# Writing a kernel's converted weights to a tile of their own in one pass, and issuing the next raw load right behind it

## The chip, the cores and the metric

The kernel runs on one core of a Trainium2 chip. The metric is the device time of one execution in microseconds (us). Engines are TensorE (PE, with its weight loads PEld), VectorE (DVE), ScalarE (ACT), GpSimd (POOL) and SyncE (SP), which here only issues DMAs.

## The reference, cut to what matters

```python
scores = np.matmul(q, k.transpose(0, 1, 3, 2)) / np.sqrt(D)        # 8 images, 8 heads, 576 x 64
scores = np.where(mask, scores + bias, -1e9)                       # window of 128 positions
attn = np.exp(scores - max); attn = attn / (attn.sum() + 1e-9)
x = np.matmul(attn, v)                                             # as 4608 x 512
h = np.maximum(np.maximum(x @ w1, x @ w2), x @ w3)                 # 512 x 768 each
out = h @ w_out                                                    # 768 x 512
```

q, k and v are 32-bit floats. The four weight matrices reach the kernel as 64-bit floats; their bits are made into 32-bit floats on the chip.

## The kernel before, in words

**Work by image.** Each of the 8 images has 18 attention steps (two heads of 128 rows each). In a step the scores are computed on PE (L431), masked and biased on DVE (L447 or L450, then L461 twice), exponentiated on ACT (L473 twice), summed and inverted (ACT L479, DVE L480), scaled on POOL (L487) or ACT (L492), transposed on PE (L500), copied out of PSUM by ACT (L504, L509 or L512), masked on POOL (L520, L524) and multiplied with v on PE (L545, later L567). ACT's L552 takes the finished head out.

The x of a finished image is cut into a high and a low part (ACT L614, DVE L615). Then PE makes the maxout products, image after image, while the attention of the next image is worked in between. Image 0 is done in 44 plain units, v = 0 to 43, each of 12 matmuls of 128x288 (L791; the first half of units 0 to 2 stands apart as L767). Four units make one of the groups g = 0 to 8 of w1, w2, w3. The results lie in three PSUM banks used in turn, so unit v can begin only when the result of unit v - 3 has been taken out: by ACT (L805) or by DVE (L808), depending on g. Image 0's units begin at about 57.5 us, and from there PE has work to the end.

**The weights.** They come in 12 sets of 128 x 1024 values in the order of `g_order`; "set n" below is the n-th in that order (sets 0, 1 and 5 to 11 serve g = 0 to 8, sets 2 to 4 the output matrix). For each set `preparing` does this:

- `fetch` (L152) loads the raw 64-bit words into one of two buffers (`raw_tile`, name hs2) over SP's queue.
- `exponents` works on the exponent bytes: one DVE pass (L166) for the first six sets, two ACT passes (L170, L171) for the others.
- `convert` makes sign and exponent with one DVE pass (L177 or L181) and joins them with the mantissa by a shift and an or (L186).
- The floats are stored to DRAM (L327, `plain`), and `part` cuts them in two steps into a high part (ACT L200) and a low part (DVE L203) in `ring` or `ow`, from which PE reads, and stores those (L216, `keep`).

In the kernel before, L186 writes the floats over the front of the raw buffer. Its output starts where the small exponents lay, and it goes in three passes of 256, 512 and 256 elements. The buffer is then free only when the floats have been stored and both parts made, and the fetch of set n + 2 is written behind the second part (L333).

**What sets the order.** Up to image 2 a scheduler decides at compile time in which order each engine takes its instructions; the events list gives only the order in which they are written. Each engine and each DMA queue then works its own list strictly in order, waiting on semaphores. What stands behind a waiting instruction waits too.

The pool of 7 buffers named hs also holds `dist`, `idle` and, from group 2 on, the cut h of an image.

Of the kernel before, what the change touches and what calls it, by code (L numbers as in the profile page):

```python
# [8 lines left out]
F32 = mybir.dt.float32  # L9
F32R = mybir.dt.float32r  # L10
I32 = mybir.dt.int32
U32 = mybir.dt.uint32
# [3 lines left out]
ALU = mybir.AluOpType  # L16
# [21 lines left out]
def attention_maxout_kernel(  # L38
# [11 lines left out]
    nc = tc.nc  # L50
    P = 128
# [3 lines left out]
    DM = H * D  # L55
    NG = w_all.shape[0]
# [12 lines left out]
    hs_p = ctx.enter_context(tc.tile_pool(name="hs_p", bufs=7))  # L69
# [21 lines left out]
    for a in range(2):  # L91
        for d in (slice(0, P),) if a == 0 else (slice(0, D), slice(D, P)):
            nc.gpsimd.affine_select(
                out=prev[d, a], in_=prev[d, a], pattern=[[1, P]], compare_op=ALU.is_gt, fill=0.0,
# [49 lines left out]
    raws = {}  # L144
    SMALL = DM // 2

    def raw_tile():
        return hs_p.tile([P, SMALL + 4 * DM], I32, name="hs2", bufs=2)

    def fetch(g):  # L150
        r = raws[g] = raw_tile()
        nc.sync.dma_start(r[:, SMALL:].bitcast(U8)[:, :16 * DM - 3], w_all[g].bitcast(U8)[:, 3:])  # L152

    def pieces(g):
        r = raws[g]
        x = r[:, SMALL:].rearrange("p (n w) -> p n w", w=2)
        sign = r[:, SMALL:].bitcast(I8).rearrange("p (n b) -> p n b", b=8)[:, :, 4]
        return x[:, :, 0], x[:, :, 1], sign, r[:, :SMALL].bitcast(I8)

    def floats(g):  # L160
        return raws[g][:, :2 * DM].bitcast(F32).rearrange("p (e w) -> p e w", e=4)

    def exponents(g, few):
        _, t, top, small = pieces(g)
        if few:
            x = nc.vector.tensor_scalar(out=small, in0=top, scalar1=-56.0, scalar2=56.0, op0=ALU.max, op1=ALU.min)  # L166
            if g == 0:
                tc.keep_in_program_order(x)
        else:
            nc.scalar.activation(small, top, AF.Relu, bias=-56.0)  # L170
            nc.scalar.activation(t.bitcast(F32), top, AF.Relu, scale=-2.0 ** 27, bias=-56.0 * 2.0 ** 27)  # L171

    def convert(g, few):
        u, t, top, small = pieces(g)
        u = u.bitcast(U32)
        if few:
            nc.vector.tensor_tensor_reduce(  # L177
                out=t, in0=top, in1=small, scale=2.0 ** 27, scalar=0.0, op0=ALU.subtract, op1=ALU.max, accum_out=None,
            )
        else:  # L180
            nc.vector.scalar_tensor_tensor(  # L181
                out=t, in0=small, scalar=2.0 ** 27, in1=t.bitcast(F32), op0=ALU.mult, op1=ALU.subtract
            )
        y = raws[g][:, :2 * DM].bitcast(U32)
        for c in (slice(0, SMALL), slice(SMALL, 3 * SMALL), slice(3 * SMALL, 4 * SMALL)):
            nc.vector.scalar_tensor_tensor(  # L186
                out=y[:, c], in0=u[:, c], scalar=5, in1=t[:, c].bitcast(U32),
                op0=ALU.logical_shift_right, op1=ALU.bitwise_or,
            )

    def sums(t, n):
        for to, a, b, op in (
# [17 lines left out]
    def part(g, n):  # L210
        e = slice(2 * n, 2 * n + 2)
        if g < 9:
            f = plain_place(g)
            hi_lo(f[:, e, 0], f[:, e, 1], floats(g)[:, e])
            k = slice(1, 4) if n else slice(0, 1)
            nc.sync.dma_start(keep[g][n][:, :k.stop - k.start], f[:, k].bitcast(F32))  # L216
        else:
            f = ow[:, slice(5, 7) if n else slice(0, 5, 4), g - 9]
            hi_lo(f[:, :, 0], f[:, :, 1], floats(g)[:, e])
# [64 lines left out]
    def ahead(n, a):  # L284
        if (n, a) in SPARE:
            return begun == B and (n < LAST + 8 or made == B)
        if n < 9 * PB:
            return n < 3 or (n - 3, 3) in used
        i = ringed[a].index(n)
        if i < 9 * PB + RING:  # L290
            return all((x, 3) in used for x in range(i - 3, i - 1))
        return i < RING or (ringed[a][i - RING], 6 if a else 3) in used
# [27 lines left out]
    g_order = [0, 1, 9, 10, 11, 2, 3, 4, 5, 6, 7, 8]  # L320

    def preparing():
        for n, g in enumerate(g_order):
            exponents(g, n < FEW)
            yield
            convert(g, n < FEW)
            nc.sync.dma_start(plain_keep[g], floats(g))  # L327
            yield
            for k in range(2):
                while g < 9 and not ahead(g, 1):  # L330
                    yield True
                part(g, k)
                if k == 1 and n + 2 < NG:  # L333
                    fetch(g_order[n + 2])
                yield

    prepared, owed = 0, 0
    steps_of_weights = preparing()

    def weights(n=0, upto=0):  # L340
# [269 lines left out]
    xs, hs, hq = {}, {}, {}  # L610
# [266 lines left out]
    for s, (t, i) in enumerate(steps):  # L877
        c = s + shift[tasks[t][0]]
# [16 lines left out]
    for t, (b, _) in enumerate(tasks):  # L895
        for e in sorted(set(MIX[t % 4])):
            c = where[t, e]
# [92 lines left out]
```

## Time and profile before

| | before |
|---|---|
| median of 3 runs | 750.51 us (749.09 to 750.65) |
| the profiled execution, its own time | 752.57 us |
| its span in the profile | 750.9 us |
| PE busy | 733.9 us, 98% of the span |
| DVE busy | 515.2 us, 69% |
| ACT busy | 487.2 us, 65% |
| POOL busy | 236.4 us, 31% |
| raw weight loads | 12 of 1023.6 KB, 7.2 us median to landing |

The span is what the profiler sees between the first and the last instruction; the time contains some launch cost around it. The profiled execution is 2.06 us above the median of the runs.

### The profile page before, as it was taken

The numbers are of one execution on the slowest core, as the hardware profiler recorded it, in microseconds if no ns is written. First come the engines' busy times: TensorE is split into PE (matmuls) and PEld (weight loads), VectorE is DVE, ScalarE is ACT, GpSimd is POOL, SyncE is SP. The second block draws the span as 40 slices with busy tenths as digits, with TensorE's granted clock in tenths as the row PEclk, the third lists the DMA queues.
The fourth block names the chain that finished last, engine by engine and source line by source line (L and its number), as shares of the span: only waits on it lengthen the run. The fifth ranks groups of instructions, "written<-read, shape, count | busy, mean of one in ns | idle before, by whom it ended". The sixth has DMA issues, their size and how long they took to land.

```text
span 750.9 us, 19281 instructions
## 1 busy us (share of the span) xinstructions
PE 733.9 (98%) x7209; PEld 674.6 (90%) x7214; DVE 515.2 (69%) x1614; ACT 487.2 (65%) x1603; POOL 236.4 (31%) x451
## 2 busy tenths in 40 slices
PE   7999989999999999999999999999999999999998
PEld 3459988999999999999999999999999999999998
DVE  4888887536659477784778567794777747683673
ACT  5786976766667767676677757776666767552342
POOL 4661224645556123212222123222222122343100
PEclk8999999999999999999999999999999999999999
DMA  7877999759998489855988378864988468899611
GB/s 252 274 282 298 330 340 331 253 187 340 361 349 275 134 279 303 273 181 192 322 294 276 116 266 304 291 213 146 330 289 273 163 228 272 252 291 355 230 61 64
DMA packets 57085, 192.81 MB, mean 257 GB/s; under 512 B 5792, under 2 KB 24480, under 8 KB 50464
## 3 DMA queue, kind: packets, MB, share of 16 engines
q0 software_dynamic: 20304, 108.54, 43.9%
q1 hardware_dynamic: 36400, 82.85, 31.2%
q8 instruction: 57, 0.93, 0.5%
q14 instruction: 36, 0.29, 0.1%
q10 hardware_dynamic: 288, 0.20, 0.1%
HBM read 156.95 MB, written 34.60 MB: 255 GB/s over the span
## 4 chain that ended last, share of the span: by engine, by line
PE 77%; DVE 11%; ACT 7%; DMA 2%; issue 1%; POOL 1%; SPq 0%; DVEq 0%; ACTq 0%; POOLq 0%
PE ps_m L846 46%; PE ps_m L791 16%; PE ps_s L431 5%; PE pt L500 4%; PE ps_x L567 4%; DVE hs L615 2%; DVE hq L733 2%; ACT p L473 2%; DVE t L732 2%; DMA qk<-in_qk 1%; PE ps_x L545 1%; DMA hs<-in_w_all 1%; ACT p L492 1%; DVE t L618 1%; DVE xs L615 1%
## 5 line engine op out<-in xcount | busy, mean ns | idle before, releaser
L846 PE MATMUL ps_m<-xs,ring 128*128 128x288 f32 x2160 | 302.7, 297 | 0.6
L846 PEld LDWEIGHTS ps_m<-xs,ring 128*128 128x128 f32 x2160 | 290.1, 188 | 3.7 <-ACT t L863 3.4
L520 POOL TENSOR_SCALAR_AFFINE_SELECT pp<-pr 128x256 f32<-128x256 f32 x112 | 53.9, 482 | 277.2 <-ACT pr L504 154.0
L473 ACT ACTIVATE p<-s,st 128x128 f32<-128x128 f32 x288 | 114.7, 400 | 20.8 <-DVE st L461 17.2
L863 ACT COPY t<-ps_m 128x288 f32<-128x288 f32 x196 | 76.7, 394 | 71.2 <-PE ps_m L846 69.5
L791 PE MATMUL ps_m<-xs,ring 128*128 128x288 f32 x846 | 118.1, 297 | 2.8 <-DVE hq L808 2.2
L791 PEld LDWEIGHTS ps_m<-xs,ring 128*128 128x128 f32 x846 | 113.3, 188 | 4.1 <-DVE hq L808 2.4
L367 POOL DMA_DIRECT2D ring<-keep x103 | 55.5, 539 | 165.5 <-PE ps_m L846 157.3
L846 PE MATMUL ps_m<-hs,ow 128*128 128x288 f32 x756 | 105.8, 297 | 0.4
L846 PEld LDWEIGHTS ps_m<-hs,ow 128*128 128x128 f32 x756 | 100.9, 188 | 2.6 <-ACT t L863 1.2
L492 ACT ACTIVATE p<-p,st 128x128 f32<-128x128 f32 x252 | 84.6, 393 | 24.1 <-DVE st L480 24.1
L732 DVE TENSOR_TENSOR t<-ps_m,t 128x288 f32<-128x288 f32 x108 | 48.8, 453 | 42.8 <-PE ps_m L846 32.5
L461 DVE CUSTOM_DVE_ANT_0 s<-ps_s,bias 128x128 f32<-128x128 f32 x240 | 60.6, 285 | 9.0 <-POOL bias_t L112 3.4
L431 PE MATMUL ps_s<-qk 64*64 64x192 f32 (+1 forms) x1088 | 62.0, 319 | 3.4 <-DMA qk<-in_qk 2.4
L614 ACT CAST hs<-hq 128x288 fp32r<-128x288 f32 x96 | 40.2, 432 | 30.8 <-DVE hq L733 18.1
L473 ACT ACTIVATION_READ_ACCUMULATOR p<-s,st 128x1 f32 x288 | 55.3, 192 | 0.0
L567 PE MATMUL ps_x<-pp,v 64*64 64x64 f32 (+3 forms) x1456 | 53.4, 274 | 0.1
L567 PEld LDWEIGHTS ps_x<-pp,v 64*64 64x64 f32 x1456 | 41.7, 133 | 10.5 <-issue 8.6
L500 PE MATMUL pt<-plus,p 128*128 128x128 f32 x288 | 48.5, 289 | 2.0 <-POOL p L487 1.3
L524 POOL TENSOR_SCALAR_AFFINE_SELECT pp<-pr 128x256 f32<-128x256 f32 (+1 forms) x112 | 50.0, 447 | 1.1
L733 DVE TENSOR_TENSOR hq<-t,hq 128x288 f32<-128x288 f32 x108 | 48.8, 457 | 2.1
L601 DVE TENSOR_TENSOR xk<-ps_x,xk 128x256 f32<-128x256 f32 (+3 forms) x56 | 25.4, 454 | 36.0 <-ACT xk L600 36.0
(94 smaller groups left out, 942.0 us busy)
## 6 DMA issues: line engine op xcount, KB each, us to landing
ring<-keep POOLq DMA_DIRECT2D x51, 1024.0 KB, 7.4
ring<-keep POOLq DMA_DIRECT2D x61, 768.0 KB, 6.1
qk<-in_qk SPq DMA_DIRECT2D x31, 576.0 KB, 5.3
hs<-in_w_all SPq DMA_DIRECT2D x12, 1023.6 KB, 7.2
v<-in_v SPq DMA_DIRECT2D x32, 320.0 KB, 6.5
outT<-t SPq DMA_DIRECT2D x64, 144.0 KB, 1.8
keep<-ring SPq DMA_DIRECT2D x9, 768.0 KB, 6.5
plain<-hs SPq DMA_DIRECT2D x12, 512.0 KB, 4.0
```

Of the source, the lines that this page charges most:

```text
L367: nc.gpsimd.dma_start(wts[n, a], keep[n % 9][a])
L431: pe(nc.tensor.matmul(ps[j][d:d + D, o:o + k1 - k0], lhsT=qkt[u][j * D:(j + 1) * D, 0, q0:q0 + D], rhs=qkt[u][j * D:(j + 1) * D, 1, k0:k1] ...
L461: first(nc.vector.tensor_tensor_reduce(out=x, in0=ps[j][:, P:2 * P], in1=below, scale=-0.125, scalar=3.0e38, op0=ALU.add, op1=ALU.min, acc ...
L473: nc.scalar.activation(p[:, j], x, AF.Exp, bias=st[:, 0, a, j:j + 1], scale=-1.0, accum_out=st[:, 1, a, j:j + 1])
L492: nc.scalar.activation(p[:, j], p[:, j], AF.Copy, scale=st[:, 2, a, j:j + 1])
L500: pe(nc.tensor.transpose(out=pt[:, a, j], in_=p[:, j], identity=ident))
L567: pe(nc.tensor.matmul(x[j * D:(j + 1) * D, r, o:o + rhs.shape[1]], lhsT=vv[k, i, j * D:(j + 1) * D], rhs=rhs[k], start=start, stop=True, s ...
L732: nc.vector.tensor_tensor(out=s, in0=ps, in1=e, op=ALU.add)
L733: nc.vector.tensor_tensor(out=h, in0=s, in1=h, op=ALU.max)
L791: pe(nc.tensor.matmul(ps, lhsT=lt, rhs=rt, start=n == 0 and not (b == 0 and v < EARLY), stop=n == len(pairs) - 1, skip_group_check=True,))
L846: pe(nc.tensor.matmul(part_of[n, {2: 0, 5: 0, 6: 0, 3: 1}.get(kk, kk)], lhsT=lt, rhs=rt, start=first, stop=i == len(pairs) - 1, skip_group ...
L863: nc.scalar.copy(out=e, in_=ps)
```

## The change

The floats get a tile of their own from the pool hs. Because nothing is overwritten now, one pass of 1024 elements takes the place of the three. The fetch of the set after the next is written directly behind the pass, ahead of the store of the floats; it has to wait only for the passes that read the raw buffer.

```diff
+    made_floats = {}
+
     def floats(g):
-        return raws[g][:, :2 * DM].bitcast(F32).rearrange("p (e w) -> p e w", e=4)
+        return made_floats[g].rearrange("p (e w) -> p e w", e=4)
...
-        y = raws[g][:, :2 * DM].bitcast(U32)
-        for c in (slice(0, SMALL), slice(SMALL, 3 * SMALL), slice(3 * SMALL, 4 * SMALL)):
-            nc.vector.scalar_tensor_tensor(
-                out=y[:, c], in0=u[:, c], scalar=5, in1=t[:, c].bitcast(U32),
-                op0=ALU.logical_shift_right, op1=ALU.bitwise_or,
-            )
+        made_floats[g] = hs_p.tile([P, 2 * DM], F32, name="hs")
+        nc.vector.scalar_tensor_tensor(
+            out=made_floats[g].bitcast(U32), in0=u, scalar=5, in1=t.bitcast(U32),
+            op0=ALU.logical_shift_right, op1=ALU.bitwise_or,
+        )
...
             convert(g, n < FEW)
+            if n + 2 < NG:
+                fetch(g_order[n + 2])
             nc.sync.dma_start(plain_keep[g], floats(g))
...
                 part(g, k)
-                if k == 1 and n + 2 < NG:
-                    fetch(g_order[n + 2])
```

The scheduler answers with another order on every engine. Three places matter below. In the changed kernel's rows the line numbers are higher by 1 (up to the fetch) or 2 to 3 within `convert` (L183 is L181 of before, L187 the one pass).

The first place is SP's list at set 0, near the program's start (plain0 and keep0 are the stores of group 0, hs2 the raw buffers). Before:

```order
L327 DMA plain0_138<-hs2_161 128x1024
L216 DMA keep0_0_120<-ring_119 128x512
L216 DMA keep0_1_121<-ring_119 128x1536
L152 DMA hs2_354<-in_w_all 128x8189
L399 DMA v_364<-in_v 128x640
```

With the change:

```order
L152 DMA hs2_335<-in_w_all 128x8189
L330 DMA plain0_138<-hs_333 128x1024
L217 DMA keep0_0_120<-ring_119 128x512
L217 DMA keep0_1_121<-ring_119 128x1536
L400 DMA v_363<-in_v 128x640
```

The load of set 2 moved from behind the three stores of set 0 to ahead of them; it is so for each later set.

The second place is DVE's list around the drain of unit v = 20 (the last row of each piece: ps_m2_1476 before, ps_m2_1466 with the change, hold that unit's result). Before, the raw buffer hs2_1087 holds set 9:

```order
L181 SCALAR_TENSOR_TENSOR hs2_1087<-hs2_1087 128x1024
L480 RECIPROCAL st_1359<-st_1359 128x4
L186 SCALAR_TENSOR_TENSOR hs2_1087<-hs2_1087 128x256
L601 TENSOR_TENSOR xk0_1219<-ps_x_1435,xk0_1219 128x256
L186 SCALAR_TENSOR_TENSOR hs2_1087<-hs2_1087 128x512
L450 COPY_PREDICATED ps_s_102<-prev_108,ps_s_102 128x2x128
L186 SCALAR_TENSOR_TENSOR hs2_1087<-hs2_1087 128x256
L461 ISA s_1472,st_1471<-ps_s_102,bias_113 128x128
...
L203 TENSOR_TENSOR ring_119<-hs2_1087,ring_119 128x2x256 x2
L461 ISA s_1474,st_1471<-ps_s_102,bias_113 128x128
...
L808 TENSOR_TENSOR hq_1181<-ps_m2_1476,hq_1181 128x288
```

With the change, hs2_1159 holds set 10:

```order
L183 SCALAR_TENSOR_TENSOR hs2_1159<-hs2_1159 128x1024
L187 SCALAR_TENSOR_TENSOR hs_1468<-hs2_1159 128x1024
L602 TENSOR_TENSOR xk0_1212<-ps_x_1425,xk0_1212 128x256
L451 COPY_PREDICATED ps_s_102<-prev_108,ps_s_102 128x2x128
L204 TENSOR_TENSOR ring_119<-hs_1468,ring_119 128x2x256
L462 ISA s_1462,st_1461<-ps_s_102,bias_113 128x128
...
L462 ISA s_1464,st_1461<-ps_s_102,bias_113 128x128
...
L204 TENSOR_TENSOR ring_119<-hs_1468,ring_119 128x2x256
L809 TENSOR_TENSOR hq_1174<-ps_m2_1466,hq_1174 128x288
```

The same work stands ahead of the drain, but it belongs to the next set: the weights run one set further ahead, and L480 has left the stretch.

The third place is ACT's list while image 0's attention is still running (ow is where set 2's parts go, pr is filled from the transposed attention, xk_445 is the finished head that L552 takes out). Before:

```order
L552 COPY xk_445<-ps_x 128x576
L473 ACTIVATE p,st<-s,st 128x128
L504 COPY pr<-pt 128x512
L200 CAST ow<-hs_354 128x2x256 x2
L473 ACTIVATE p,st<-s,st 128x128 x2
L479 ACTIVATE st<-st 128x4
```

With the change:

```order
L553 COPY xk_445<-ps_x 128x576
L201 CAST ow<-hs 128x2x256 x2
L474 ACTIVATE p,st<-s,st 128x128 x2
L505 COPY pr<-pt 128x512
L480 ACTIVATE st<-st 128x4
```

The two casts of set 2 and one more exponential now stand ahead of the copy of the transposed attention.

## Rows read from the trace of the kernel before

**Rows 1.** Busy time by stretch: PE, PEld, DVE, ACT, POOL; clock, DMA share, GB/s.
```profile
97.00:123.33 26.33, 22.43 (x247) 20.25 (x245) 21.67 (x63) 20.84 (x60) 9.35 (x15) 1.00 0.93 329
123.33:751.00 627.67, 623.11 (x6203) 593.32 (x6201) 417.89 (x1304) 394.70 (x1308) 186.28 (x362) 1.00 0.74 248
```

**Rows 2.** Timeline of PE: start, length, instructions, idle before them.
```profile
42.85 2.66 PE L767 MATMUL ps_m<-xs,ring 128*128 128x288 f32 x18 [0.18 <-DVE xs L615]
...
57.52 4.27 PE L791 MATMUL ps_m<-xs,ring 128*128 128x288 f32 x30 [0.63 <-DVE xs L615]
...
96.94 5.03 PE L791 MATMUL ps_m<-xs,ring 128*128 128x288 f32 x36
104.14 1.86 PE L791 MATMUL ps_m<-xs,ring 128*128 128x288 f32 x12 [2.17 <-DVE hq L808]
...
115.02 0.88 PE L431 MATMUL ps_s<-qk 64*64 64x192 f32 x16 [0.95 <-DVE st L461]
...
122.73 0.84 PE L500 MATMUL pt<-plus,p 128*128 128x128 f32 x4 [0.64 <-ACT p L492]
```

**Rows 3.** Timeline of DVE around the drain of unit 20.
```profile
98.50 1.23 DVE L181 SCALAR_TENSOR_TENSOR hs<-hs 128x1024 int32<-128x1024 int8 x1 [2.11 <-ACT hs L171]
...
102.01 1.49 DVE L203 TENSOR_TENSOR ring<-hs,ring 128x512 fp32r<-128x512 f32 x2
...
103.64 0.45 DVE L808 TENSOR_TENSOR hq<-ps_m,hq 128x288 f32<-128x288 f32 x1
```

**Rows 4.** Timeline of ACT: the exponent passes of sets 6, 7 and 9.
```profile
67.91 1.15 ACT L170 ACTIVATE hs<-hs 128x1024 int8<-128x1024 int8 x1 [1.32 <-DMA hs<-in_w_all]
...
78.09 1.15 ACT L170 ACTIVATE hs<-hs 128x1024 int8<-128x1024 int8 x1 [0.46 <-DMA hs<-in_w_all]
...
97.36 1.11 ACT L171 ACTIVATE hs<-hs 128x1024 f32<-128x1024 int8 x1
```

**Rows 5.** The page's group of exponentials: count | busy, mean ns | idle before.
```profile
L473 ACT ACTIVATE p<-s,st 128x128 f32<-128x128 f32 x288 | 114.7, 400 | 20.8 <-DVE st L461 17.2
```

**Rows 6.** Waits of SP's queue to 140 us: total, times, longest.
```profile
SPq L152 <- DMA plain<-hs: 15.7, 8, 3.2
```

**Rows 7.** The raw loads (line L152), from issue to landing.
```profile
DMA to landing us min/median/max: 5.0/7.2/10.7
```

**Rows 8.** Timeline of DVE: passes of set 1 and what follows the first.
```profile
28.25 0.42 DVE L186 SCALAR_TENSOR_TENSOR hs<-hs 128x256 uint32<-128x256 uint32 x1
28.58 0.29 DVE L447 COPY_PREDICATED ps_m<-prev,ps_m 128x128 f32<-128x128 uint8 x1
28.78 0.68 DVE L186 SCALAR_TENSOR_TENSOR hs<-hs 128x512 uint32<-128x512 uint32 x1
```

**Rows 9.** Timeline of ACT in image 0's attention.
```profile
38.43 0.57 ACT L504 COPY pr<-pt 128x512 f32<-128x512 f32 x1
38.89 1.14 ACT L200 CAST ow<-hs 128x512 fp32r<-128x512 f32 x2
...
45.76 0.59 ACT L504 COPY pr<-pt 128x512 f32<-128x512 f32 x1
```

**Rows 10.** Timeline of DVE in image 0's attention.
```profile
33.51 0.69 DVE L166 TENSOR_SCALAR hs<-hs 128x1024 int8<-128x1024 int8 x1
...
34.41 1.28 DVE L177 CUSTOM_DVE_ANT_0 hs<-hs 128x1024 int32<-128x1024 int8 x1
...
47.39 0.18 DVE L480 RECIPROCAL st<-st 128x4 f32<-128x4 f32 x1
...
56.30 1.17 DVE L615 TENSOR_TENSOR xs<-xk,xs 128x576 fp32r<-128x576 f32 x1
```

**Rows 11.** Timeline of POOL in image 0's attention.
```profile
34.56 1.40 POOL L524 TENSOR_SCALAR_AFFINE_SELECT pp<-pr 128x256 f32<-128x256 f32 x1
...
39.43 0.41 POOL L524 TENSOR_SCALAR_AFFINE_SELECT pp<-pr 128x256 f32<-128x256 f32 x1
...
49.60 0.61 POOL L487 TENSOR_TENSOR p<-p,st 128x256 f32<-128x256 f32 x1
```

## The prediction

> **What bounds the kernel now.** I first read the busy times by stretch. From 123.33 us to the end PE is busy for 623.11 of 627.67 us at a granted clock of 1.00, full speed; nothing the change touches runs there, so that part moves as one block. Between 97 and 123.33 us PE is busy for only 22.43 of 26.33 us, and this is where the weights are still being made [rows 1]. So the time is: when image 0's units begin (57.52 us), plus PE's work, plus what PE waits after that.
>
> PE's timeline names these waits. There are three between 57.52 and 123.33 us: 2.17 us before unit 23, released by DVE's L808; 0.95 us before a score block, released by DVE's L461; 0.64 us before a transposition, released by ACT's L492 [rows 2]. Together they are 3.76 us, the most that the later stretch can give. PE also waited 0.63 us just before 57.52 us.
>
> The timeline of DVE says why unit 23 waits. Unit 23 needs the bank of unit 20, whose drain ran at 103.64 us, although PE began units 20 to 22 at 96.94 us. The drain stood behind the whole of set 9: DVE sat idle for 2.11 us for ACT's exponent pass L171, ran L181 at 98.50 us, then the passes, two L203 from 102.01 us, and only then the drain [rows 2, 3]. The exponent pass on ACT, at 97.36 us, waited for no load. But ACT and DVE release each other in turn from 78 us on, and that round began late: ACT waited for raw loads, 1.32 us for set 6 and 0.46 us for set 7 [rows 4]. The loads were late because SP held them behind the stores: the raw fetch waited 15.7 us in 8 waits for the store of the floats [rows 6].
>
> **The change part by part.**
>
> *One pass for three.* A pass of 256 elements takes 0.42 us, and the next instruction starts 0.33 us after it; one of 512 takes 0.68 us, of which I count 0.60 us to the next start by the same overlap [rows 8]. That makes 0.27 us per 256 elements and 0.06 us fixed, so 1024 elements in one pass cost about 1.14 us of DVE against 0.33 + 0.60 + 0.33 = 1.26 us. It saves 0.12 us a set, 1.4 us in 12 sets. L181, an operation of the same kind on 1024 elements, took 1.23 us with its tail [rows 3], which agrees. Only the sets ahead of a PE wait can hand it on: I count two of them, 0.2 us. The lower bound is nothing (DVE waits for ACT in the round anyhow), the upper 0.4 us.
>
> The first cast of a set (ACT L200) needed only two of the passes before and needs all of the one now. But other work stood between the passes, and L480 and L601 leave that stretch in the new order, so I cost it at nothing.
>
> *Two tiles instead of one.* The new tile comes from the pool hs. By then the cut h of group 2 takes four of its seven buffers. A pass could wait for the store of an older set's floats, but the sets come some 10 us apart (67.91 and 78.09 us [rows 4]), and with three buffers left the store has two sets' time to land. I cost it at nothing; if a store took longer than that, the pass and every drain behind it on DVE would wait for the rest.
>
> *The earlier fetch.* It passes the store of its set's predecessor and, for ring sets, two keep stores. Those stores stand one instruction further back, and nobody waits for them before image 1. The load takes 5.0 to 10.7 us [rows 7] and now starts when the raw words were last read, not when the floats have been stored and cut. ACT's two waits for loads, 1.32 and 0.46 us, go. More than that: the order shows that with the loads in time the scheduler puts the weights one whole set ahead. Where set 9 stood ahead of unit 20's drain, set 10 stands now; set 11, which was made from 114 us on, takes the place of set 10, and behind it no weights are left.
>
> *What this does to PE's waits.* The second and third wait, 0.95 and 0.64 us, lay where DVE and ACT made sets 10 and 11. With set 11 a place earlier, ACT and DVE have only attention and drains there, and I let both waits go: -1.59 us. The first wait stays in part, since a set still stands ahead of unit 20's drain. The round on ACT and DVE begins 0.46 us earlier (no wait for the load) and loses some 0.2 us by the merged passes, and behind L181 only one exchange with ACT is left ahead of the drain, where L480, an extra pass and a second exchange stood. From L181's start to the drain was 103.64 - 98.50 = 5.14 us; without the passes' 0.12 us and one L480 and wait I take 4.6 us. So the drain comes 0.46 + 0.54 = 1.0 us earlier, and the first wait falls from 2.17 to about 1.2 us. Bounds: nothing (the round is paced by something else) and the whole 2.17 us.
>
> *What it does to the start.* The new order also brings weights forward into image 0's attention, and here it costs. Set 2's two casts, 1.14 us [rows 9], and one exponential, 0.40 us [rows 5], now stand ahead of ACT's L504, which ran at 38.43 us: this copy comes 1.5 us later. On DVE all of set 3 (L166 0.69, L177 1.28, the pass 1.14 us [rows 8, 10]) moves ahead of the last score steps, which come some 3 us later. Three things give back. The 18 matmuls of L767, 2.66 us, stood ahead of a transposition and now stand behind it [rows 2], so the next L504 (45.76 us [rows 9]) comes earlier. The last L480 ran at 47.39 us, but POOL's L487, which needs it, only at 49.60 us [rows 10, 11]: 2.2 of the 3 us are slack. And the last L615, at 56.30 us, no longer waits behind L480 [rows 10]. I take +0.3 us for the start, between -0.6 us (PE's own 0.63 us wait ahead of 57.52 us is all that can go) and +3 us (the whole delay of DVE's steps).
>
> *The sum.* -1.0 (first wait) - 1.6 (the other two) + 0.3 (start, which PE may in part lose again in its first wait) = -2.3 us. The profiled execution goes from 752.57 to 750.3 us. The runs shown have their median 2.06 us below it, so I forecast 750.51 - 2.3 = **748.2 us**.
>
> **A rule that speaks against it.** POOL's L524 took 1.40 us where it met DVE's L177 (34.41 to 35.69 us), and 0.41 us where it met no such pass [rows 10, 11]. It ended just behind L177: POOL stood still for the length of the DVE pass. The Trainium skill (SBUF — State Buffer, "SBUF: two separate sides") says why: a DVE instruction with two SBUF inputs and a GpSimd instruction that reads SBUF exclude each other for the whole of the instruction. By the row as by the rule, one pass of 1.14 us can hold POOL for 0.5 us longer than the longest of the three, 0.60 us. In image 0's attention POOL is often on the chain; if each of sets 0 to 4 meets it, the start comes 5 x 0.5 = 2.5 us later and the sum is about nothing. I hold it a rival and not the forecast, since the pass meets only what POOL happens to do then.
>
> **The rivals.**
>
> *The start is late by one to two us and the later waits shrink by no more* (POOL held as above, or L504's 1.5 us not made good). For it: the rows above, and that the rounds after 57.52 us follow the start. Against it: PE's wait at unit 23 absorbs a late start as long as the drain is not late too. -2.6 + 1.5 to 2.5 gives -1.1 to -0.1 us, about **749.9 us**. That the earlier loads buy nothing at all (the round is paced otherwise) would give 750.3 us and belongs here too.
>
> *Slower: set 3 ahead of the last score steps.* The place is DVE between 38 and 48 us, the price the 3 us by which image 0's last steps come later, plus one or two POOL operations held for 1 us as at 34.56 us. If this reaches 57.52 us undiminished and the drains follow it, the change is +3 to +5 - 2.6 us, at 752 us. It decides from a start later than about 61.6 us (57.52 + 2.6 + 1.5). For it: the moved rows on ACT and DVE. Against it: 2.2 us of slack at POOL's L487, and L767 out of the way.
>
> **How the numbers follow.** A measurement of this kernel tells some 0.2% (1.5 us) from no change. The forecast, 747 to 749 us, gets 0.60, the first rival 0.26, the slower one 0.12; 0.02 remain for more than the 3.76 us of waits. The forecast's case lies almost wholly beyond -1.5 us: faster 0.61, same 0.26, slower 0.13. The range reaches from all three waits gone and a start earlier by 0.5 us (746.2 us) to a little beyond no change (751.1 us), which leaves out most of the slower case and the best tail.
>
> **What would show it.** Right: no wait of ACT's L170 for a load; raw fetches of sets 6 and 7 issued some 8 to 12 us earlier; one 1.2 us pass a set; the wait at unit 23 near 1 us; no PE wait near 114 and 122 us; the first L791 within 1 us of 57.52 us. The forecast is wrong if the first L791 comes after 59 us, if PE waits at new places between 60 and 100 us (a pass waiting for a buffer of hs, or ACT's L170 for a load that lands late), or if unit 20's drain still ends at 104 us.

## The result, and the profile after

The changed kernel takes 756.54 us (median of 5 runs, 753.77 to 757.99) beside 749.43 us of the kernel before (median of 5 runs; two runs more than stood ahead of the prediction). The ratio is 1.0087, 95% interval 1.0062 to 1.0112; here and below it is worked out over all runs and is not the quotient of the two medians. Measured again (`after_again`, below), it was 1.0078 [1.0051, 1.0106]. The change is slower by 0.8 to 0.9%, some 5 to 7 us.

In the changed kernel the lines behind the diff have other numbers: the pass is L187, the exponent passes on ACT L172 and L173, the first DVE pass L183, the casts L201; otherwise a line is 1 higher than before (L504 is L505, L487 is L488, L791 is L792, L808 is L809). The profiled execution took 753.77 us, the least of the five. Its busy time by stretch, in the columns of [rows 1]:

```profile
97.00:123.33 26.33, 23.30 (x260) 21.03 (x259) 20.63 (x65) 21.57 (x68) 10.33 (x19) 1.00 0.85 318
123.33:751.00 627.67, 624.41 (x6235) 594.62 (x6233) 417.82 (x1303) 394.31 (x1304) 185.79 (x362) 1.00 0.74 247
```

PE is busier by 0.87 us between 97 and 123.33 us than before. PE's timeline, as in [rows 2]:

```profile
60.28 4.27 PE L792 MATMUL ps_m<-xs,ring 128*128 128x288 f32 x30
...
98.16 1.06 PE L568 MATMUL ps_x<-pp,v 64*64 64x192 f32 x22 [0.58 <-POOL pp L521]
...
107.25 1.86 PE L792 MATMUL ps_m<-xs,ring 128*128 128x288 f32 x12 [1.91 <-DVE hq L809]
...
116.04 0.80 PE L568 MATMUL ps_x<-pp,v 64*64 64x192 f32 x16 [0.17 <-POOL pp L521]
117.21 0.34 PE L568 MATMUL ps_x<-pp,v 64*64 64x64 f32 x6 [0.38 <-POOL pp L521]
```

Image 0's units begin at 60.28 us, 2.76 us later. The wait at unit 23 fell only from 2.17 to 1.91 us; the other two of [rows 2] are gone but for 0.55 us, and a new one of 0.58 us stands at 98.16 us. DVE at that place, as in [rows 3], and the exponent passes that waited for loads, as in [rows 4]:

```profile
101.88 1.23 DVE L183 SCALAR_TENSOR_TENSOR hs<-hs 128x1024 int32<-128x1024 int8 x1 [0.56 <-ACT hs L173]
103.14 1.23 DVE L187 SCALAR_TENSOR_TENSOR hs<-hs 128x1024 uint32<-128x1024 uint32 x1
...
106.75 0.45 DVE L809 TENSOR_TENSOR hq<-ps_m,hq 128x288 f32<-128x288 f32 x1
```

```profile
80.35 1.15 ACT L172 ACTIVATE hs<-hs 128x1024 int8<-128x1024 int8 x1 [0.81 <-DMA hs<-in_w_all]
...
88.73 1.13 ACT L172 ACTIVATE hs<-hs 128x1024 int8<-128x1024 int8 x1 [0.32 <-DMA hs<-in_w_all]
```

The pass takes 1.23 us, and the next instruction on DVE starts 1.14 us after it (104.28 us), as costed. The fetches of sets 6 and 7 went out at 54.20 and 61.74 us, 8.6 and 8.9 us earlier, but ACT still waits for loads, now at sets 8 and 9. The loads' times to landing, as in [rows 7], have grown:

```profile
DMA to landing us min/median/max: 6.2/8.1/12.7
```

**The two profiles are not alike at the start.** The first matmuls behind PE's wait for q and k ran at half the clock in the profile of before (a view as in [rows 2]: 14 score matmuls in 1.34 us; the granted clock reads 0.50 from 12 to 16 us) and at full clock in this one (0.77 us; 1.00):

```profile
11.26 1.34 PE L431 MATMUL ps_s<-qk 64*64 64x192 f32 x14 [2.41 <-DMA qk<-in_qk]
```

```profile
11.07 0.77 PE L432 MATMUL ps_s<-qk 64*64 64x192 f32 x14 [2.35 <-DMA qk<-in_qk]
```

That is luck of the execution, since a second profile of the same changed kernel (`after_again`) had the slow start too. It put this profile about 3.2 us ahead at 34 us. The units start 2.76 us late in spite of it, so image 0's attention lost about 6 us. The second profile is the fair one to compare.

### The profile page after: what moved, and what is told of

Read it like the earlier page. It is cut to its first block, busy times and chain, and to the rows that moved or that the text cites. A ratio compares the mean times of both kernels' runs of the same rounds, so it can differ in the third digit from the quotient of the medians.

```text
span 752.1 us, 19259 instructions
## 1 busy us (share of the span) xinstructions
PE 731.1 (97%) x7209; PEld 673.6 (90%) x7214; DVE 512.6 (68%) x1590; ACT 487.0 (65%) x1603; POOL 236.2 (31%) x451
## 4 chain that ended last, share of the span: by engine, by line
PE 77%; DVE 9%; ACT 5%; DMA 4%; POOL 2%; issue 2%; SPq 0%; DVEq 0%; ACTq 0%; POOLq 0%
PE ps_m L847 46%; PE ps_m L792 16%; PE ps_x L568 5%; PE ps_s L432 5%; PE pt L501 4%; DVE hs L616 2%; DMA hs<-in_w_all 2%; DMA qk<-in_qk 2%; DVE hq L734 2%; DVE t L733 2%; ACT p L474 1%; POOL pp L525 1%; DMA plain<-hs 1%; DVE t L619 1%; ACT p L493 1%
## 5 line engine op out<-in xcount | busy, mean ns | idle before, releaser
L792 PE MATMUL ps_m<-xs,ring 128*128 128x288 f32 x846 | 117.5, 297 | 1.9 <-DVE hq L809 1.9
L792 PEld LDWEIGHTS ps_m<-xs,ring 128*128 128x128 f32 x846 | 113.2, 188 | 2.7 <-DVE hq L809 2.1
L432 PE MATMUL ps_s<-qk 64*64 64x192 f32 (+1 forms) x1088 | 60.2, 317 | 2.5 <-DMA qk<-in_qk 2.3
L451 DVE COPY_PREDICATED ps_s<-prev,ps_s 128x256 f32<-128x256 uint8 x105 | 44.4, 423 | 8.4 <-PE ps_s L432 6.8
```

Of the source, the lines that this page charges most:

```text
L432: pe(nc.tensor.matmul(ps[j][d:d + D, o:o + k1 - k0], lhsT=qkt[u][j * D:(j + 1) * D, 0, q0:q0 + D], rhs=qkt[u][j * D:(j + 1) * D, 1, k0:k1] ...
L792: pe(nc.tensor.matmul(ps, lhsT=lt, rhs=rt, start=n == 0 and not (b == 0 and v < EARLY), stop=n == len(pairs) - 1, skip_group_check=True,))
```

## The experiments

Four theories: the **order** theory (the scheduler's new order puts weights ahead of attention on ACT and DVE, and PE waits), the **POOL** theory (the longer pass holds POOL longer), the **contention** theory (earlier loads land late), and the theory that the clock alone makes the difference. "A", "B" and "C" in the first expectations are the first three. All runs of one paragraph shared a chip with the kernel before. "Idle" is PE's idle time in the profile, from the windows 36 to 58 us (before: 1.9) and 58 to 138 us (before: 3.9). It does not hold what a fallen clock costs: between 58 and 138 us the mean granted clock was 1.00 in the profiles of before, `after_again`, `small_t`, `hold_74_pin`, `hold_74_late` and `hold_74_both`, and 0.94 to 0.98 in the other eleven. A mean of 0.98 over 80 us is worth about 1.6 us (0.02 x 80), by my estimate.

| run | median us | before | ratio [95%] | idle 36-58, 58-138 |
|---|---|---|---|---|
| one_late | 754.58 | 751.64 | 1.0029 [1.0010, 1.0049] | 2.9, 3.3 |
| three_early | 753.51 | 751.64 | 1.0019 [1.0000, 1.0038] | 4.0, 2.9 |
| three_late | 754.22 | 751.64 | 1.0038 [1.0020, 1.0056] | 3.2, 3.9 |
| early_from4 | 753.42 | 751.64 | 1.0027 [1.0004, 1.0050] | 1.9, 5.4 |
| after_again | 756.89 | 752.12 | 1.0078 [1.0051, 1.0106] | 5.9, 4.4 |
| hold_front | 755.64 | 752.12 | 1.0050 [1.0028, 1.0071] | 2.7, 5.1 |
| hold_74 | 754.99 | 752.12 | 1.0042 [1.0027, 1.0056] | 2.4, 4.2 |
| hold_74_three | 756.41 | 752.12 | 1.0063 [1.0043, 1.0083] | 1.4, 5.5 |
| small_t | 755.04 | 751.63 | 1.0043 [1.0024, 1.0063] | 1.5, 4.6 |
| own_pool | 769.02 | 751.63 | 1.0219 [1.0195, 1.0243] | 5.3, 6.2 |
| own_pool_held | 766.50 | 751.63 | 1.0190 [1.0151, 1.0229] | 2.0, 8.2 |
| own_pool_held_three | 770.12 | 751.63 | 1.0234 [1.0208, 1.0259] | 2.6, 11.3 |
| hold_74_pin | 752.62 | 752.77 | 0.9997 [0.9979, 1.0015] | 1.6, 3.8 |
| hold_74_late | 755.24 | 752.77 | 1.0034 [1.0017, 1.0050] | 2.2, 5.3 |
| pin_weights | 760.41 | 752.77 | 1.0101 [1.0061, 1.0141] | 5.2, 3.6 |
| hold_74_both | 752.96 | 752.67 | 1.0007 [0.9987, 1.0027] | 2.2, 2.1 |

### The parts of the change, one by one

`one_late` leaves the load at its old place (first lines below), `three_early` keeps three passes (last line), `three_late` does both, so that only the new tile is left; `early_from4` issues loads early only from set 4 on.

```diff
-            if n + 2 < NG:
-                fetch(g_order[n + 2])
...
                 part(g, k)
+                if k == 1 and n + 2 < NG:
+                    fetch(g_order[n + 2])
...
+        for c in (slice(0, SMALL), slice(SMALL, 3 * SMALL), slice(3 * SMALL, 4 * SMALL)):
```

> The new tile and the single pass, with the next raw load issued where it was before, behind the set's second part. Theory A (the earlier load lets the scheduler bring weights forward into image 0's attention, and the units start late): the loss goes, 748.5 to 750 us, first plain unit within 1 us of 57.52 us. Theory B (one pass of 1.2 to 1.6 us holds POOL longer than three short ones, and POOL is on the chain in image 0's attention): as slow as the full change, 754 to 757 us, with POOL operations of 1.3 to 1.5 us beside the pass. Theory C (loads issued earlier meet other transfers and land late): 749 to 750 us, ACT waits for no load longer than before.

> The new tile and the earlier load, but three passes instead of one. Theory A: as slow as the full change, 754 to 757 us, units start 2 to 6 us late. Theory B: back to 748 to 750 us. Theory C: as slow as the full change, with waits of ACT or DVE for raw loads after 60 us rather than a late start.

> The new tile alone: three passes, and the load at its old place. All three theories: no change, 748.5 to 750.5 us. A loss here would mean that the tile's place in the pool hs, or the order that follows from it (the second pass no longer has to wait for the words it overwrites), costs by itself, which none of them holds.

> The full change, but the loads that sets 0 to 3 issue stay at their old place; from set 4 on the next load is issued right behind the pass. Theory A: the front is as before, and the later waits still shrink: 746.5 to 749 us, first unit within 1 us of 57.52 us. Theory B: as slow as the full change, 754 to 757 us, since the front's passes are still single. Theory C: part of the loss stays, 751 to 755 us, as the later loads are the ones that land late (set 9 took 12.7 us).

All four lie between the two kernels, 1.8 to 2.9 us above before, and no theory fits all four. `one_late` came within the POOL theory's range and `early_from4` within the contention theory's, but every theory gave `three_late` no change, and it is 2.6 us slower. The tile alone costs as much as the others. The scheduler gave each of the four another order, and each has its own PE waits. In `early_from4` the front is as good as before's, but ACT waits for a load at 67.80 us, and PE pays behind it (line numbers are 1 and 3 higher there than in the changed kernel: an exponent pass, and a transposition):

```profile
67.80 1.13 ACT L173 ACTIVATE hs<-hs 128x1024 int8<-128x1024 int8 x1 [2.33 <-DMA hs<-in_w_all]
```

```profile
74.89 0.66 PE L504 MATMUL pt<-plus,p 128*128 128x128 f32 x4 [2.85 <-POOL p L491]
```

No single edit was undone here without a new order. So the next runs hold the order itself.

### Holding the order of the kernel before

`after_again` is the changed kernel. In `hold_front` and `hold_74` its first DVE, ACT and POOL instructions are chained, issue order only, in the sequence they have in the kernel before; `hold_74_three` does that with three passes. The lists of PE and of the DMA queues are not held.

```diff
+    def hold(name, table):
+        here = [i for i in tc.nc.cur_bb.bb.instructions if str(i.engine).endswith("." + name)]
...
+        for a, b in zip(order, order[1:]):
+            tc.add_manual_dep(here[b], here[a].name, mybir.DependencyInfo(
+                mybir.DependencyClass.NoSync, mybir.DependencyReason.DATA), reason="order")
```

> The changed kernel unaltered, beside the holds below and on their chip. If the waits of PE in image 0's attention are the cause, it stays 3 to 6 us slower than the kernel before; the runs should spread over some 5 us with the mean granted clock, about 0.75 us for each 0.001 of it, since the clock falls behind PE's waits in some executions and not in others.

> The full change (own tile, one pass, early load), with the order of DVE, ACT and POOL held to that of the kernel before up to the first units of image 0 (100 instructions of DVE, 111 of ACT, 59 of POOL); behind that the order is free. Order theory (it is the new order of weights and attention in image 0's attention that makes PE wait 7.0 instead of 1.9 us between 36 and 58 us): these waits go back to 2 to 3 us, the units start as in the kernel before with the same clock, and 748 to 751 us result, unless the free order behind makes new waits. POOL theory (the single pass holds POOL, whatever the order): the waits in the front stay above 4 us and 753 to 757 us result.

> As the run with the held front, but held on to about 74 us of the kernel before (135 instructions of DVE, 140 of ACT, 62 of POOL). Order theory: 747.5 to 751 us, front waits 2 to 3 us, and no wait of over 1 us before 97 us; any gain over the kernel before is then that of the waits behind 97 us. POOL theory: 753 to 757 us.

> As the run held to 74 us, but with three passes into the new tile instead of one (149 instructions of DVE held). Order theory: the same as the run held to 74 us within 1 us. POOL theory: 2 to 4 us faster than it, since the three short passes hold POOL for less at a time.

`after_again` shows the front undisguised. PE's timeline:

```profile
41.83 1.02 PE L376 MATMUL pt<-hs 128*128 128x512 bf16 x4 [1.62 <-ACT pr L505]
...
44.76 0.65 PE L546 MATMUL ps_x<-pp,v 128*64 128x256 f32 x4 [1.33 <-POOL pp L521]
47.18 0.66 PE L501 MATMUL pt<-plus,p 128*128 128x128 f32 x4 [1.77 <-POOL p L488]
48.51 1.33 PE L376 MATMUL pt<-hs 128*128 128x512 bf16 x3 [0.67 <-ACT pr L505]
...
50.81 3.42 PE L768 MATMUL ps_m<-xs,ring 128*128 128x288 f32 x18
...
64.85 1.32 PE L792 MATMUL ps_m<-xs,ring 128*128 128x288 f32 x8
```

What stood ahead of these, on ACT, DVE and POOL:

```profile
39.39 1.14 ACT L201 CAST ow<-hs 128x512 fp32r<-128x512 f32 x2
...
41.21 0.57 ACT L505 COPY pr<-pt 128x512 f32<-128x512 f32 x1
```

```profile
41.46 0.69 DVE L168 TENSOR_SCALAR hs<-hs 128x1024 int8<-128x1024 int8 x1
...
42.34 1.24 DVE L179 CUSTOM_DVE_ANT_0 hs<-hs 128x1024 int32<-128x1024 int8 x1
43.46 0.98 DVE L616 TENSOR_TENSOR xs<-xk,xs 128x576 fp32r<-128x576 f32 x1
44.37 1.42 DVE L187 SCALAR_TENSOR_TENSOR hs<-hs 128x1024 uint32<-128x1024 uint32 x1
```

```profile
42.37 1.46 POOL L525 TENSOR_SCALAR_AFFINE_SELECT pp<-pr 128x256 f32<-128x256 f32 x1
43.80 0.91 POOL L521 TENSOR_SCALAR_AFFINE_SELECT pp<-pr 128x256 f32<-128x256 f32 x1
44.66 1.38 POOL L525 TENSOR_SCALAR_AFFINE_SELECT pp<-pr 128x256 f32<-128x256 f32 x1
46.03 1.10 POOL L488 TENSOR_TENSOR p<-p,st 128x256 f32<-128x256 f32 x1
```

The two casts of set 2 make the copy L505 late, and PE waits 1.62 us. Set 3's three DVE passes and the cuts L616 then run almost back to back beside POOL's masks, and these four POOL operations take 4.85 us. With the order held, and the single pass in it, the same four take 2.72 us in `hold_74`, as in the kernel before:

```profile
39.44 0.41 POOL L525 TENSOR_SCALAR_AFFINE_SELECT pp<-pr 128x256 f32<-128x256 f32 x1
39.80 0.85 POOL L521 TENSOR_SCALAR_AFFINE_SELECT pp<-pr 128x256 f32<-128x256 f32 x1
40.61 0.85 POOL L525 TENSOR_SCALAR_AFFINE_SELECT pp<-pr 128x256 f32<-128x256 f32 x1
41.56 0.61 POOL L488 TENSOR_TENSOR p<-p,st 128x256 f32<-128x256 f32 x1
...
47.55 1.40 POOL L525 TENSOR_SCALAR_AFFINE_SELECT pp<-pr 128x256 f32<-128x256 f32 x1
```

(The last one, beside set 3's single pass, took 0.61 us in the kernel before; no PE wait follows it.) PE's idle time in the front goes back from 5.9 to 2.4 us, and to 1.4 us with three passes. So the front's loss is the order; the length of the pass can explain at most the 1.0 us between the last two.

But the time falls less: from 1.0078 to 1.0050 and 1.0042, within the range that the POOL theory gave (753 to 757 us), though its two signs, front waits above 4 us and three passes 2 to 4 us faster, did not come. New waits stand behind the held part. In `hold_74`, ACT and then PE:

```profile
72.18 1.14 ACT L172 ACTIVATE hs<-hs 128x1024 int8<-128x1024 int8 x1 [1.26 <-DMA hs<-in_w_all]
73.22 0.36 ACT L510 COPY pp<-pt 128x256 f32<-128x256 f32 x1
73.48 1.14 ACT L173 ACTIVATE hs<-hs 128x1024 f32<-128x1024 int8 x1
74.50 0.38 ACT L513 COPY pr<-pt 128x256 f32<-128x256 f32 x1
```

```profile
77.39 0.71 PE L501 MATMUL pt<-plus,p 128*128 128x128 f32 x4 [2.17 <-POOL p L488]
```

The scheduler put set 7's exponent pass ahead of the attention's copies, as if its load had landed; on the chip it had not, ACT stood still, and the attention stood behind it. In `hold_front` the same pass waited 2.83 us at 72.56 us.

PE's wait is no longer than that of the kernel before at 104.14 us (2.17 us), and PE idles only 0.3 us more behind 58 us (4.2 against 3.9). What differs most is the clock behind the wait, half (0.50) in `hold_74` and full in the kernel before:

```profile
78.00:80.00 2.00, 2.00 (x8) 1.43 (x8) 2.00 (x7) 0.95 (x4) 0.00 (x0) 0.50 0.96 250
```

```profile
104.00:106.00 2.00, 1.86 (x16) 1.70 (x19) 1.97 (x9) 2.00 (x7) 0.00 (x0) 1.00 0.96 199
```

I held no more than 74 us with this tile: floats and the cuts of h share the pool hs, whose buffers are handed out in program order, and in the order of before a later pass comes behind an earlier cut.

### A pool of its own

To hold the whole order, the floats got a one-buffer pool (`fl`), paid for with six instead of ten buffers of the small tiles t. `small_t` is the control: the kernel before with six.

```diff
-    t_p = ctx.enter_context(tc.tile_pool(name="t_p", bufs=10))
+    fl_p = ctx.enter_context(tc.tile_pool(name="fl_p", bufs=1))
+    t_p = ctx.enter_context(tc.tile_pool(name="t_p", bufs=6))
...
+        made_floats[g] = fl_p.tile([P, 2 * DM], F32, name="fl")
```

> Control: the kernel before with six instead of ten buffers of the small tiles t, which pays for a 4 KB buffer in the next three kernels; the order on every engine is that of the kernel before. All theories: no change, within 0.2% of the kernel before.

> The full change, with the floats in a one-buffer pool of their own instead of the pool hs (six buffers of t); the order is left to the scheduler. Order theory: the scheduler again mixes weights into the attention in a new way, and 751 to 757 us result, by its luck. Pool theory (the cuts of h and the floats share hs, whose buffers are given out in program order, so the passes must run ahead of later cuts, and this alone makes the order bad): 747 to 750 us.

> As the run with the pool of its own, and the whole order of DVE, ACT and POOL held to that of the kernel before (one pass in the place of the second of three). Only durations and loads differ from before. Order theory: not slower than the kernel before, 748 to 751.5 us (ratio 0.996 to 1.001): the one pass saves 0.1 us a set, and ACT's waits for loads, 1.3 and 0.5 us, go. POOL theory (the longer pass holds POOL): 753 to 756 us, with PE waits on POOL in the front. Contention theory (earlier loads collide with other transfers): 752 to 755 us, with waits for DMA.

> The same with three passes. Order theory: within 1 us of the held run with one pass (up to 1 us slower). POOL theory: 2 to 4 us faster than the held run with one pass. Contention theory: as slow as that.

All four expectations missed, and these runs are no test of the theories. The control costs 3.4 us by itself. With one buffer the pass waits for the store of the floats before it, 0.2 to 3.4 us in 7 sets of the held run:

```profile
95.07 1.22 DVE L188 SCALAR_TENSOR_TENSOR fl<-hs 128x1024 uint32<-128x1024 uint32 x1 [3.37 <-DMA plain<-fl]
```

That wait blocks DVE's whole queue, and PE then waited 3.87 us at 99.73 us. The prediction named this price; in the profile of the changed kernel itself no pass waits for a store.

### Moving only the exponent passes, only the load

`hold_74_pin` is `hold_74` with ACT's exponent passes (sets 6 to 11; the expectation says 5 to 11) tied behind what precedes them in the program. `hold_74_late` is `hold_74` with the load at its old place; there the exponent pass stands, by the instructions' order, where `hold_74_pin` has it. `pin_weights` ties the weights on ACT and DVE in the changed kernel, except for the first DVE pass of sets 6 to 11 (L183) and the low parts (L204), with nothing held.

```diff
-            nc.scalar.activation(small, top, AF.Relu, bias=-56.0)
+            tc.keep_in_program_order(nc.scalar.activation(small, top, AF.Relu, bias=-56.0))
```

> The run held to 74 us, with one more tie: ACT's two exponent passes of a set (sets 5 to 11) may not be put ahead of ACT instructions that stand before them in the program. In the run held to 74 us the exponent pass of set 7 stood ahead of two copies, an exponential and a scaling of the attention, waited 1.26 us for its raw load at 72.18 us, and PE then waited 2.17 us at 77.39 us. Order theory: this PE wait falls under 0.5 us, and the time falls by 1.5 to 3 us, to 752 to 753.5 us beside a kernel before of 752 us, unless waits behind 100 us grow. Contention theory (the loads themselves are late, wherever ACT waits): the PE wait stays above 1.5 us and the time within 1 us of the run held to 74 us.

> The run held to 74 us, with the next load issued at its old place, behind the set's second part; one pass, own tile. By the instructions' order the exponent pass of set 7 then stands behind the attention's copies, as in the kernel before. Order theory: no PE wait above 0.5 us at 77 us, 751.5 to 753.5 us. POOL theory (the single pass): 753.5 to 756 us.

> The full change with every DVE and ACT instruction that makes weights tied behind what stands ahead of it in the program on its engine; no order is taken from the kernel before. Order theory: PE's waits between 36 and 58 us fall from 6 to 7 us to 2 to 4 us, and 750 to 754 us result, against 757 us of the change; waits behind 97 us may grow, since weights now come later. If the waits stay as they are (755 us or more), the harm of the order is not that weights pass attention that stands before them in the program.

`hold_74_pin` came out as the order theory said: no PE wait at 77 us (the longest near it is 0.53 us, at 80.40 us), and no loss against before, 0.9997. `hold_74_late` came out 1.7 us above the order theory's range and within the POOL theory's; but its single pass is in `hold_74_pin` too, which loses nothing. Here the pass waits for its later load, and the next copy L505 behind it reaches POOL and PE late:

```profile
77.39 1.14 ACT L172 ACTIVATE hs<-hs 128x1024 int8<-128x1024 int8 x1 [2.41 <-issue]
```

```profile
82.54 0.33 PE L568 MATMUL ps_x<-pp,v 64*64 64x64 f32 x2 [2.40 <-POOL pp L521]
```

The profile names no releaser for that 2.41 us, but it is the load. It was issued at 70.10 us, 3.5 us later than in `hold_74_pin` (66.62 us), and landed 7.2 us later, just ahead of the pass:

```profile
DMA to landing us min/median/max: 7.2/7.2/7.2
```

The two runs differ by 0.37 of a per cent. Up to about 83 us the orders of ACT and POOL are the same in both, and DVE's but for one drain, so there the early load saves PE about 2 us of waiting (2.40 against 0.53 us); behind that the orders differ too (`hold_74_late` has another wait of 2.12 us at 102.62 us), so the whole difference is not shown to be the load's. `pin_weights` is a miss: it has another poor order, with 5.2 us of waits in the front, and a mean granted clock of 0.989 against 0.996 of the kernel before. By its own expectation the harm is then not that weights pass attention written ahead of them; what makes that order poor stays open.

`hold_74_both` ties also the casts written behind unit 8 and the DVE pass L183 of sets 8 to 11 (the expectation says 5 to 11), which in `hold_74_pin` stood ahead of a score step at 95.29 us:

```profile
95.29 1.23 DVE L183 SCALAR_TENSOR_TENSOR hs<-hs 128x1024 int32<-128x1024 int8 x1 [1.30 <-ACT hs L173]
```

> The run with the held front and the tied exponent passes, and behind 60 us also the casts of the weights (ACT) and the first DVE pass of sets 5 to 11 tied behind what stands ahead of them in the program. In the run without these ties DVE's first pass of a set stood ahead of a score step at 95.29 us, waited 1.30 us for ACT, and PE waited 1.33 us at 101.12 us; now the score step stands ahead of it. Order theory: that wait falls under 0.5 us, the time falls by another 0.5 to 1.5 us, and the version beats the kernel before by 0.5 to 1.5 us (ratio 0.998 to 0.9995), the first that does. Otherwise: within 0.2% of the kernel before, or slower by a new wait elsewhere.

The wait fell only from 1.33 to 0.98 us. Over the stretch PE's idle time is 2.1 us against 3.9 us of before:

```profile
58.00:138.00 80.00, 77.92 (x817) 70.90 (x816) 62.83 (x175) 60.85 (x178) 25.95 (x46) 1.00 0.95 331
```

```profile
58.00:138.00 80.00, 76.10 (x817) 70.36 (x816) 64.07 (x189) 60.38 (x177) 24.51 (x45) 1.00 0.91 330
```

(`hold_74_both` above, the kernel before below.) Its span was 749.7 us against 750.9 us, but that profile also ran less of its start at half clock (mean 0.95 against 0.91 up to 36 us), and the medians are level: 1.0007 [0.9987, 1.0027]. No version beat the kernel before by more than the interval can tell.

## Why the prediction was wrong

**The forecast was 748.2 us. The step that failed is "What it does to the start": +0.3 us, with +3 us as its bound.** By `after_again`, which like the profile of before ran the first matmuls at half clock, the front costs 6.5 us: the same score matmuls start 0.8 us later at 32 us (32.89 against 32.09 us), and the first unit 7.3 us later (64.85 against 57.52 us). PE's idle time in that stretch grew by 6.0 us, from 2.1 to 8.1 us, and its busy time by 0.5 us. The first profile of the changed kernel has the same length of it, though it began at full clock. Before, `after_again`, and the first profile:

```profile
32.09:57.52 25.43, 23.34 (x186) 13.01 (x187) 21.62 (x69) 20.63 (x72) 14.74 (x22) 1.00 0.79 274
```

```profile
32.89:64.85 31.96, 23.85 (x187) 13.44 (x188) 25.52 (x70) 21.43 (x72) 14.98 (x21) 0.95 0.81 284
```

```profile
28.32:60.28 31.96, 23.81 (x188) 13.28 (x189) 25.52 (x70) 21.45 (x72) 14.99 (x21) 0.95 0.83 303
```

Behind the waits the granted clock fell to half (0.50 from 50 to 52 us in `after_again`), and the 18 matmuls of L768 took 3.42 us instead of 2.66 us [rows 2]. Three of the prediction's own signs of being wrong came: a first unit behind 59 us, a PE wait at a new place below 100 us (98.16 us), and unit 20's drain behind 104 us (106.75 us).

- *The copy 1.5 us later* was about right: L505 ran behind the two casts, 2.0 us later when the 0.8 us are taken off, and PE's wait there grew from 0.55 to 1.62 us.
- *2.2 of DVE's 3 us are slack* was wrong. The slack at L487 [rows 11] was counted with POOL's operations at their old lengths. With the changed order they ran beside set 3's passes and took 4.85 us instead of 2.72 us, and PE waited 1.33 us and 1.77 us where before it waited nothing.
- *L767 moved behind a transposition gives back* was wrong: PE stood idle at the transposition instead (the 1.77 us), and did L768 later. The 0.63 us wait just ahead of the units did go.

**The rule.** POOL beside DVE's two-input passes took 1.46 us and 1.38 us for an operation of 0.41 to 0.85 us. The trace agrees with the rule of the Trainium skill (SBUF — State Buffer, "SBUF: two separate sides") that the prediction weighed. Its form in the prediction, five passes each 0.5 us longer, is not what happened: in the old order (`hold_74`) the single pass left those four POOL operations as they were and lengthened one other, at 47.55 us, by 0.8 us without a PE wait. The order brought the passes next to POOL's work. The row that the prediction set against it, L524 with 0.41 us at 39.43 us, was not free of such a pass: DVE's low part L203, an operation of two inputs, began 0.1 us behind it, at 39.55 us.

**The rivals.** The slower one had the right place and mechanism (set 3 on DVE ahead of the last score steps, held POOL operations behind it). Its threshold, a start after 61.6 us, was passed in `after_again` (64.85 us) and not in the first profile with its lucky start (60.28 us); 752 us was too small, as was the first rival's 749.9 us.

**The later waits: forecast -2.6 us.** From the first unit to the end `after_again` won back 1.6 us (7.3 us late at the first unit, spans of 756.6 and 750.9 us). The two later waits went but for 0.4 us, and one of 0.5 us came at 102.61 us. The first fell by 0.26 us instead of 1.0 us: a set still stands ahead of unit 20's drain, and L183 to the drain took 106.75 - 101.88 = 4.87 us, not 4.6 us.

**The earlier loads.** Issued 8.6 and 8.9 us earlier, as forecast. "ACT's waits for loads go" was wrong in kind: with an early load the scheduler put the exponent pass earlier in ACT's queue. In the changed kernel ACT's waits were 0.81 and 0.32 us; in `hold_front`, `hold_74` and `early_from4` 2.83, 1.26 and 2.33 us, each with attention behind them.

**The passes and the tile.** One pass of 1.23 us: right, except beside POOL's work (1.42 us at 44.37 us). "The new tile costs nothing" was right for the buffers and wrong for the time: the tile alone (`three_late`) cost 0.38%. It gave the scheduler another order, which I take to be the reason; no run shows that.

**What is shown and what is not.** Shown: with the order of before in the front and the exponent passes behind the attention, the same tile, single pass and early load cost nothing (0.9997 [0.9979, 1.0015] beside 1.0078). They don't gain either: the forecast's ratio, 0.997, lies outside that interval. Not shown: that each single-edit run loses for the same reason; their waits were read but not taken away one by one. The share of the clock is an estimate, and it is not apart from the order, since in `after_again` and `hold_74` the clock fell behind waits that the order made: 112 runs of the kernel before, on three chips, average 750.9 us where the granted clock was 0.998 or more (37 runs), 752.2 us at 0.995 to 0.997 (59) and 753.6 us at 0.994 or less (16), about 0.45 us for each 0.001. The changed kernel averaged 0.993 in 11 runs against 0.996, which makes 1.2 us of its 5 us.

## What to carry to other kernels

Where a scheduler sets the order, an edit that makes side work ready earlier is first an edit of the order: compare the orders, and look for side work that now stands ahead of the chain that feeds the bounding engine, above all for an instruction in an in-order queue that waits for a load. Slack read from the old trace holds only while its neighbours keep their lengths. To learn whether an edit or the order costs, hold the old order and run the edit in it.

## What the runs showed of the hardware

- The same kernel's executions differ by more than 5 us on one chip (before: 748.1 to 754.9 us in its 56 runs on the chip of `small_t` and of the runs below it in the table), and the mean granted clock goes with it, as above. One profile shows one draw of this: the first profile of the changed kernel was only 1.2 us above before's, its median 7 us.
- A half-clock stretch can be missing from the profile's clock column: in `after_again` the column says 1.00 from 10 to 18 us, but 14 score matmuls took 1.34 us, as in the half-clock stretch of before, not 0.77 us. So a mean granted clock can be read too high: that run has 0.997.
- The length of a wait does not tell whether the clock falls behind it: behind 2.17 us of PE's waiting it fell to 0.50 in `hold_74` and stayed at 1.00 in the kernel before, in the rows above.
- Four fewer buffers of a 288-element tile cost 3.4 us (`small_t`); in its profile the longest new waits of PE, 2.1 us for ACT and DVE, stand near the end:

```profile
677.68 2.65 PE L846 MATMUL ps_m<-hs,ow 128*128 128x288 f32 x18 [0.51 <-ACT t L716]
...
683.52 1.45 PE L846 MATMUL ps_m<-hs,ow 128*128 128x288 f32 x9 [1.57 <-DVE t L718]
```
